# Eight products moved from the output stretch to the weights' stretch of a convolution and spectral-mix kernel

## The chip, the cores and the metric

One core of a Trainium2 chip. The metric is the device time of one execution in microseconds, as the median of several runs. A program on one core has no second die to compare with, so a run counts as slow only when it is over 1.5% above the fastest of its kernel. A ratio is the mean time of one kernel's fast runs over the mean time of the other's fast runs of the same rounds, so it is not quite the ratio of the medians beside it. Brackets hold its 95% interval.

## The reference

```python
# x: 8 x 3264 x 192.  u = causal convolution of x with 7 softmax-ed taps per head
X = np.fft.rfft(u, axis=1)                      # 64 modes are kept
Yr = einsum(Xr, w_r) - einsum(Xi, w_i)          # one 192 x 192 matrix per mode
Yi = einsum(Xr, w_i) + einsum(Xi, w_r)
y = np.fft.irfft(Y, n=S, axis=1)
v = u + y
out = v + np.maximum(v @ w_ch, 0.0)
```

## The kernel before

The kernel has three stretches. Input and convolution fill `xall` (u) and `cc` (u transposed, for the product with `w_ch`). Then 16 groups of weights are loaded, and each is multiplied as it lands. Then the output is made in double tiles, called items: 128 rows of positions by 2 x 2 x 192 values, in one of four PSUM buffers. Item n uses buffer n % 4. The parts that matter:

```python
    def c_part(n, ks=(0, 1)):            # twelve products: u @ w_ch of item n
        duo, zt = items[n]
        for k, (q, t) in enumerate(duo):
            for j in range(3) if k in ks else ():
                for i, r in enumerate(ROWS):
                    nc.tensor.matmul(zt[:, i, D * k:D * k + D], cc[r, q, 3 * t + j, :], wc[r, j, :],
                                     start=(k == 0 and j == 0), stop=False, skip_group_check=True)
    # m_part(n, 0): four products, adds y @ w_ch.   relu(n): ACT, in place in PSUM.
    # m_part(n, 1): four products, adds y.          finish(n): DVE adds u, POOL stores.
    ...
    for n in range(N + 1):
        if is_duo(n):
            m_part(n, 0)
            relu(n)
        if n + 2 < N and duos[n + 2] == ("h",):          # one tile of halves, made earlier
            nc.scalar.copy(out=items[n + 2][1]..., in_=halves...)
        if n + 1 < N and n > 0:
            if is_duo(n + 1):
                if duos[n + 1] != ("h",):
                    c_part(n + 1)
            else:
                ...                                      # a spectral item: y of the next quarter
        if is_duo(n - 1):
            m_part(n - 1, 1)
            finish(n - 1)
```

The names below follow this: c(n) is `c_part`, m(n,0) and m(n,1) are the first and second products of item n.

## Time and profile before

| | before |
|---|---|
| time, median of 3 runs | 179.58 us (179.52 to 180.19) |
| span of the profiled run, mean granted clock | 178.0 us, 0.984 |
| last group of weights used by PE | 106.93 us |
| first products of item 15 | 125.51 us |
| last store issued | 172.22 us |

Read it by stretches. Up to 107 us the weights set the pace, and PE has gaps. After it PE has none but the 0.25 us in front of the tile of halves, and everything else follows PE. The lines for both stand in the prediction. The rows of the last group of weights and of the last store cut the time into pieces that can be compared between kernels: what comes before the output, the output from the last group of weights to the last store issued (172.22 - 106.93 = 65.29 us), and what is left to land (178.0 - 172.22 = 5.8 us).

### The profile page before, as it was taken

To read this page: it belongs to the slowest core of one execution; us is meant where nothing else is said; L and a number is where in the kernel's file an instruction comes from. 1 tells how busy PE (TensorE), PEld (TensorE's weight loads), DVE (VectorE), ACT (ScalarE), POOL (GpSimd) and SP (SyncE) were. 2 spreads that over 40 slices of the span, in tenths; PEclk is the share of its full clock that TensorE was granted. 3 is DMA by queue.
4 is the path that set the end of the run, shared out by engine and by line. 5 is a ranking of instruction groups with operands and counts; after the bars stand their busy time and mean duration, and the time that the engine had idled before them with its cause. 6 is when DMAs were issued, how large, how long until landed. Compare 5 with 4: busy or idle time off the path is not lost.

```text
span 178.0 us, 6299 instructions
## 1 busy us (share of the span) xinstructions
PE 146.5 (82%) x2736; PEld 105.9 (59%) x2736; DVE 114.1 (64%) x163; ACT 99.5 (56%) x136; POOL 100.4 (56%) x155
## 2 busy tenths in 40 slices
PE   0047569999999999689967679999999999999930
PEld 0033346667666666467756556965777777777720
DVE  1878555675765576255454453796688888888870
ACT  8176653735553734365546355767766667766620
POOL 7999997867855624354226100035364766665760
PEclk9999987999999999999999999999999999999997
DMA  4999999999999999999999980296699899998894
GB/s 44 168 177 188 189 190 190 192 193 190 191 191 190 205 206 208 205 206 208 205 207 206 206 130 0 90 324 258 251 300 351 317 368 356 354 349 348 336 356 186
DMA packets 44331, 40.17 MB, mean 226 GB/s; under 512 B 28800, under 2 KB 40656, under 8 KB 44304
## 3 DMA queue, kind: packets, MB, share of 16 engines
q0 software_dynamic: 41136, 37.59, 106.0%
q1 hardware_dynamic: 3168, 2.19, 3.9%
q8 instruction: 21, 0.34, 0.7%
q14 instruction: 6, 0.05, 0.1%
HBM read 39.40 MB, written 20.05 MB: 334 GB/s over the span
## 4 chain that ended last, share of the span: by engine, by line
DMA 33%; POOL 32%; PE 16%; issue 13%; ACT 1%; POOLq 1%; DVE 1%; DVEq 0%
DMA arena<-in_moe_w_i_dram 19%; POOL out_dram L586 17%; POOL xall L151 10%; DMA xall<-in_x_dram 8%; DMA cc<-in_moe_w_i_dram 6%; PE z L307 4%; PE low L333 3%; PE za L522 2%; PE za L502 2%; POOL xall L221 1%; POOL arena L428 1%; PE zb L522 1%; PE zb L502 1%; ACT xall L325 1%; PE low L387 1%
## 5 line engine op out<-in xcount | busy, mean ns | idle before, releaser
L586 POOL DMA_DIRECT2D out_dram<-arena x45 | 33.9, 754 | 39.2 <-DVE arena L578 38.4
L151 POOL DMA_DIRECT2D xall<-in_x_dram x48 | 38.5, 813 | 6.7 <-DMA xall<-in_x_dram 4.6
L307 PE MATMUL z<-xall,band 64*64 64x192 bf16 (+3 forms) x816 | 27.8, 264 | 16.1 <-ACT band L195 10.5
L327 DVE CAST xall<-z 128x768 bf16<-128x768 f32 (+1 forms) x24 | 24.5, 1021 | 15.1 <-PE z L307 13.3
L307 PEld LDWEIGHTS <-band 64*64 64x64 bf16 x816 | 18.4, 111 | 24.8 <-ACT band L195 10.9
L325 ACT CAST xall<-z 128x768 bf16<-128x768 f32 (+1 forms) x24 | 20.4, 851 | 22.3 <-PE z L307 21.1
L502 PEld LDWEIGHTS <-cc 64*128 64x128 bf16 x600 | 26.2, 94 | 7.0 <-issue 1.2
L578 DVE TENSOR_TENSOR arena<-za,xall 128x768 f32<-128x768 f32 x26 | 24.8, 956 | 5.6 <-ACT zb L553 1.9
L553 ACT ACTIVATE za<-za 128x768 f32<-128x768 f32 (+1 forms) x27 | 21.0, 782 | 8.3 <-PE za L522 8.3
L578 DVE TENSOR_TENSOR arena<-zb,xall 128x768 f32<-128x768 f32 x23 | 21.9, 956 | 4.6 <-ACT za L553 1.8
L553 ACT ACTIVATE zb<-zb 128x768 f32<-128x768 f32 (+1 forms) x25 | 19.6, 782 | 8.4 <-PE zb L522 8.2
L333 PE MATMUL low<-xall,ftab 128*128 128x384 bf16 x100 | 21.7, 344 | 0.0
L387 PEld LDWEIGHTS <-xall 128*128 128x128 bf16 x300 | 18.7, 105 | 3.2 <-issue 0.3
L362 DVE COPY cc<-r 128x1024 bf16<-128x1024 bf16 (+2 forms) x18 | 11.2, 658 | 12.8 <-PE r L387 3.9
L502 PE MATMUL za<-wc,cc 64*128 64x192 bf16 x318 | 17.8, 243 | 0.0
L522 PE MATMUL za<-mixa,fsin 64*128 64x384 bf16 (+1 forms) x120 | 17.6, 304 | 0.0
L522 PE MATMUL za<-mixa,ftab 64*128 64x384 bf16 (+1 forms) x120 | 17.6, 304 | 0.0
L428 POOL DMA_DIRECT2D arena<-in_moe_w_r_dram x12 | 7.4, 615 | 15.4 <-PE low L439 10.3
L522 PE MATMUL zb<-mixa,ftab 64*128 64x384 bf16 (+1 forms) x100 | 15.6, 313 | 0.4 <-ACT zb L553 0.4
L502 PE MATMUL zb<-wc,cc 64*128 64x192 bf16 x282 | 15.6, 243 | 0.1
L522 PE MATMUL zb<-mixa,fsin 64*128 64x384 bf16 (+1 forms) x100 | 15.6, 313 | 0.0
L522 PEld LDWEIGHTS <-ftab 64*128 64x128 bf16 x220 | 11.0, 94 | 4.6 <-issue 1.7
(111 smaller groups left out, 184.2 us busy)
## 6 DMA issues: line engine op xcount, KB each, us to landing
out_dram<-arena POOLq DMA_DIRECT2D x45, 384.0 KB, 4.3
xall<-in_x_dram POOLq DMA_DIRECT2D x24, 192.0 KB, 7.4
xall<-in_x_dram POOLq DMA_DIRECT2D x16, 240.0 KB, 7.1
arena<-in_moe_w_r_dram POOLq DMA_DIRECT2D x12, 288.0 KB, 9.6
arena<-in_moe_w_i_dram POOLq DMA_DIRECT2D x12, 288.0 KB, 10.5
out_dram<-arena SPq DMA_DIRECT2D x9, 192.0 KB, 2.1
xall<-in_x_dram POOLq DMA_DIRECT2D x8, 144.0 KB, 7.1
cc<-in_moe_w_r_dram POOLq DMA_DIRECT2D x4, 288.0 KB, 11.5
```

What stands on the lines that cost most here:

```text
L151: nc.gpsimd.dma_start(out=xall[:, s0:s0 + nf, i, :], in_=src)
L307: mm = nc.tensor.matmul(ov[c], band[r, h, c.start + shift + 64 * (r is UP and c is LO): c.start + shift + 64 * (r is UP and c is LO) + 64] ...
L325: nc.scalar.copy(out=dst, in_=srcv)
L327: nc.vector.tensor_copy(out=dst, in_=srcv)
L333: nc.tensor.matmul(xp, ftab[:, t, :], xall[:, slot(q, t), :, :], start=(t == 0), stop=False, skip_group_check=True)
L362: nc.vector.tensor_copy(out=out, in_=in_)
L387: nc.tensor.transpose(tp[:, P * k:P * k + P], src, ident[:])
L502: nc.tensor.matmul(zt[:, i, D * k:D * k + D], cc[r, q, 3 * t + j, :], wc[r, j, :], start=(k == 0 and j == 0), stop=False, skip_group_check ...
L522: nc.tensor.matmul(zt[:, i, D * k:D * (k + w)], tabs[c][r, t, :], zw[r, q:q + w, c, QUARTERS[which], :], start=False, stop=end and k + w = ...
L553: nc.scalar.activation(out=zt[:, :, 0:w], in_=zt[:, :, 0:w], func=ACT.Relu)
L578: nc.vector.tensor_tensor(out=o[:, :, :].rearrange("p k (i d) -> p i k d", i=2), in0=zt[:, :, 0:2 * D].rearrange("p i (k d) -> p i k d", k=2),
L586: nc.gpsimd.dma_start(out=dst, in_=ov)
```

## The change

Intent: in the weights' stretch PE has time to spare, in the output it has none. So c of eight items is made in the first and used in the second. The results need room: each pair has one in `band` or a slice of the arena and one in the place of columns of `cc` that are used up. ACT brings each into PSUM two items ahead. The places for stores move to make room, and `cc` and `band`, which stores now leave from, are aligned to 256 B.

```diff
-    cc = sb("cc", [NQ, CB, P], BF16)
+    cc = sb("cc", [NQ, CB, P], BF16, align_bytes=256)
-    band = sb("band", [H, 2 * P], BF16)
+    band = sb("band", [H, 2 * P], BF16, align_bytes=256)
...
+    def c_ahead(n):
+        duo = duos[n]
+        zs = []
+        for i in range(2):
+            next_bank()
+            zs.append(ring[(tbank[0] - 1) % len(ring)])
+        ...                                    # the twelve products, into two banks of the ring
+        for i in range(2):
+            copy(AHEAD[n][:, i, :, :], zs[i][:, 0:2 * D].rearrange("p (k d) -> p k d", k=2))
...
+    FREED = {8: (16,), 9: (20,), 12: (24, 28), 13: (33, 41), 14: (37, 45)}
+    free = [in_cc[0], slices[4], slices[5], in_cc[1], slices[3]]
+    LATER = {11: (in_cc[2], in_cc[3]), 15: (in_band,), 23: (slices[0],), 32: (slices[1],), 40: (slices[2],)}
...
-    PLAN = (2, 2, 1, 2, 2, 2, 1, 2, 3, 3, 3, 3, 3, 3, 99)
+    PLAN = (2, 2, 3, 2, 3, 2, 2, 2, 3, 3, 3, 3, 99, 99, 99)
...
         some(PLAN[g], NT * (NQ - 1) if g < NW + NL - 1 else NT * NQ)
+        for n in FREED.get(g, ()):
+            c_ahead(n)
...
+        if n + 2 in AHEAD:
+            nc.scalar.copy(out=four(items[n + 2][1][:, :, 0:2 * D]), in_=AHEAD[n + 2])
...
-                if duos[n + 1] != ("h",):
+                if duos[n + 1] != ("h",) and n + 1 not in AHEAD:
                     c_part(n + 1)
```

More of the change, by code (lines that the diff above doesn't have):

```diff
@@ L95, in wbuf, with place, four @@
         return wts[g] if g < NW + NL else wts[(g - NW - NL) % NW]
-    NO = 6
     OB = 2 * 2 * 2 * D
-    outs = [arena[:, OB * i:OB * (i + 1)].bitcast(F32).rearrange("p (k d) -> p k d", k=2) for i in range(NO)]
-    assert NO * OB <= NW * WGB
-    outs.append(band[:, :, :].rearrange("p h c -> p (h c)")[:, 0:OB].bitcast(F32).rearrange("p (k d) -> p k d", k=2))
+    assert 6 * OB <= NW * WGB and OB == 12 * P
+    def place(a):
+        return a.bitcast(F32).rearrange("p (k d) -> p k d", k=2)
+    def four(a):
+        return a.rearrange("p k (i d) -> p k i d", i=2)
+    slices = [place(arena[:, OB * i:OB * (i + 1)]) for i in range(6)]
+    in_band = place(band[:, :, :].rearrange("p h c -> p (h c)")[:, 0:OB])
+    in_cc = [place(cc[:, q, t:t + 12, :].rearrange("p k s -> p (k s)")) for t in (0, 12) for q in range(2)]
+    ccf = cc[:, :, :, :].rearrange("p q (t j) s -> p q t (j s)", j=3).bitcast(F32)
     pos = [0]
@@ L495, in c_halves @@
             copy(halves[:, 2 * k:2 * k + 2, :], z[:, 0:2 * D].rearrange("p (a d) -> p a d", a=2))
+    def c_ahead(n):
[4 more added lines that the diff above has]
+            zs.append(ring[(tbank[0] - 1) % len(ring)])
+        for k, (q, t) in enumerate(duo):
+            for j in range(3):
+                for i, r in enumerate(ROWS):
+                    nc.tensor.matmul(zs[i][:, D * k:D * k + D], cc[r, q, 3 * t + j, :], wc[r, j, :],
+                                     start=(k == 0 and j == 0), stop=(k == 1 and j == 2), skip_group_check=True)
+        for i in range(2):
+            copy(AHEAD[n][:, i, :, :], zs[i][:, 0:2 * D].rearrange("p (k d) -> p k d", k=2))
     def c_part(n, ks=(0, 1)):
@@ L543 @@
         duos.insert(k, item)
-    buffers = []
-    for duo in duos:
-        buffers.append(NO if duo == ("h",) else sum(b < NO for b in buffers if b is not None) % NO
-                       if isinstance(duo, tuple) else None)
+    AHEAD = {}
+    for (n1, n2), p1 in zip(((16, 20), (24, 28), (33, 37), (41, 45)), [in_band] + slices):
+        (q, t1), (_, t2) = duos[n1][0], duos[n2][0]
+        AHEAD[n1], AHEAD[n2] = four(p1), ccf[:, q:q + 2, t1:t2 + 1:t2 - t1, :]
+        assert duos[n1] == ((q, t1), (q + 1, t1)) and duos[n2] == ((q, t2), (q + 1, t2)) and (q or t1 > 7)
+    FREED = {8: (16,), 9: (20,), 12: (24, 28), 13: (33, 41), 14: (37, 45)}
+    free = [in_cc[0], slices[4], slices[5], in_cc[1], slices[3]]
+    LATER = {11: (in_cc[2], in_cc[3]), 15: (in_band,), 23: (slices[0],), 32: (slices[1],), 40: (slices[2],)}
+    buffers = []
+    for n, duo in enumerate(duos):
+        for p in LATER.get(n, ()):
+            free.insert(0, p)
+        buffers.append(None)
+        if isinstance(duo, tuple):
+            buffers[n] = free.pop(0)
+            free.append(buffers[n])
     def relu(n):
@@ L556, in finish @@
         duo, zt = items[n]
-        o = outs[buffers[n]]
+        o = buffers[n]
         if duo[0] == "h":
```

## The prediction

> **What bounds the kernel now.** I read the mean clock first (0.984, nothing to correct), then the page's 40 slices and the chain that ended last. They show three stretches: input and convolution up to about 57 us, the weights up to 107 us, the output up to 176 us. I then asked for busy times by stretch, since the change takes work from the third and puts it in the second.
>
> ```profile
> core 0: us, PE busy (x) PEld busy (x) DVE busy (x) ACT busy (x) POOL busy (x), PEclk, DMA share, GB/s
> 80.00:90.00 10.00, 9.17 (x176) 7.13 (x176) 5.32 (x11) 5.07 (x10) 3.50 (x6) 1.00 1.21 206
> 90.00:100.00 10.00, 7.29 (x140) 6.33 (x138) 4.23 (x9) 5.09 (x8) 4.70 (x8) 1.00 1.21 207
> 100.00:107.00 7.00, 4.79 (x96) 3.51 (x97) 3.67 (x7) 3.48 (x7) 0.00 (x0) 1.00 0.92 151
> 141.00:146.00 5.00, 5.00 (x94) 3.95 (x92) 4.25 (x5) 3.44 (x5) 3.43 (x5) 1.00 0.98 374
> 156.00:161.00 5.00, 5.00 (x95) 3.95 (x92) 4.25 (x5) 3.56 (x5) 3.43 (x5) 1.00 0.89 342
> ```
>
> In the weights' stretch the DMA engines are full at 206 GB/s and PE has 0.83 + 2.71 + 2.21 = 5.75 us to spare. In the output PE never rests, while DVE is busy 4.25 of 5 us, ACT 3.5, and the DMA moves 342 to 374 GB/s at shares of 0.89 to 0.98. The chain that ended last names the stores on POOL there, but POOL waits 38.4 us for DVE, which waits for ACT, which waits for PE; the timeline of one tile shows the order.
>
> ```profile
> start us, us, engine line op out<-in xcount [idle before <-releaser]
> 149.79 0.33 PE L522 MATMUL za<-mixa,ftab 64*128 64x384 bf16 x2
> 149.95 0.33 PE L522 MATMUL za<-mixa,fsin 64*128 64x384 bf16 x2
> 150.05 0.96 DVE L578 TENSOR_TENSOR arena<-zb,xall 128x768 f32<-128x768 f32 x1 [0.19 <-ACT zb L553]
> 150.12 0.66 PE L502 MATMUL za<-wc,cc 64*128 64x192 bf16 x12
> 150.32 0.80 ACT L553 ACTIVATE za<-za 128x768 f32<-128x768 f32 x1 [0.35 <-PE za L522]
> ...
> 151.26 0.66 PE L502 MATMUL zb<-wc,cc 64*128 64x192 bf16 x12
> ```
>
> For double tile n, PE runs the four first-quarter products of n, the twelve products with c of n+1, and the four second-quarter products of n-1. From one twelve to the next is 151.26 - 150.12 = 1.14 us; start to start, the twelve take 150.61 - 150.12 = 0.49 us and each four 0.33 us, so 0.33 + 0.49 + 0.33 = 1.15 us. The stage goes at PE's pace.
>
> The kernel already has one tile whose product with c was made earlier, the tile of halves (item 14): ACT copies it into PSUM, and PE then adds to it. This is what the change makes of eight more.
>
> ```profile
> 122.05 0.33 PE L522 MATMUL za<-mixa,ftab 64*128 64x384 bf16 x2
> ...
> 122.64 0.80 ACT L553 ACTIVATE za<-za 128x768 f32<-128x768 f32 x1 [0.34 <-PE za L522]
> ...
> 123.38 0.80 ACT L643 COPY zb<-cc 128x768 f32<-128x768 f32 x1
> ...
> 124.23 0.36 PE L514 MATMUL zb<-mixa,ftab 64*64 64x384 bf16 x4 [0.25 <-ACT zb L643]
> ```
>
> PE stood 0.25 us waiting for that copy: the copy came after the ReLU of item 12 on ACT, and that ReLU waited for item 12's first products. So products, ReLU, copy, products is a chain of 124.23 - 122.05 = 2.18 us over two items, whatever PE has to do meanwhile.
>
> **What the Trainium skill says.** "Perfetto Trace Analysis", section Identifying the Most-Contended Engine, warns that a busy PE is not a PE at its roofline. Hence the starts above instead of the busy share. "ScalarE: Activation LUTs", section What ACT_TABLE_LOAD costs, gives an activation with immediates as 186 ns + 0.833 ns per element, with 93 ns of overlap back to back: 826 ns for 768 elements, 733 ns apart. The trace agrees: 0.78 to 0.80 us for one, 123.38 - 122.64 = 0.74 us apart. "DMA: Bandwidth & Descriptors", section How a descriptor splits into AXI transactions, says that a descriptor which doesn't start at a multiple of 256 B costs one more partial transaction. In the kernel before as built, the arena is aligned, and cc and band start 64 B past such a multiple. But of the stores only the halves come from there, and the weights' DMA time doesn't show it (below). The same page, section Where 436 GB/s comes from, puts the HBM limit of a core at about 358 GB/s; the trace shows 374 GB/s over 5 us at share 0.98, so I take 374 / 0.98 = 382 GB/s as the ceiling (an estimate from that row).
>
> **The change part by part.**
>
> Output stretch. Removed: twelve products with c for each of items 16, 20, 24, 28, 33, 37, 41, 45, so 8 x 0.49 = 3.9 us of PE. Added on ACT: eight copies of 128x768 from SBUF to PSUM at 0.74 to 0.80 us, 6.2 us. Built, the new order has each copy after the ReLU of the item two before, exactly as in the tile of halves. For a group of four items ACT then has 5 x 0.77 = 3.9 us and DVE 4 x 0.956 = 3.8 us, less than four tiles take, so neither is a bound by sum. The order is what matters. Let S be the start of item a-2's first products. Its ReLU starts at S + 0.53 (149.79 to 150.32), the copy 0.74 later, takes 0.80, and PE goes on 0.05 after it (124.18 to 124.23): item a starts at S + 2.12. The copy also needs the DVE addition of item a-4, which frees its PSUM buffer: it starts at S + 0.26 (150.05), ends at S + 1.22, and with the 0.09 us that ACT needed after DVE elsewhere (121.62 to 121.71) the copy starts at S + 1.31, making it S + 2.16. In the kernel before the two items take 2 x 1.145 = 2.29. PE's own work would allow 2.29 - 0.49 = 1.80. So each c made ahead saves about 0.15 us and not 0.49; the other 0.34 becomes a wait of PE for ACT. After the wait, ACT is one ReLU late, done at about S + 2.9, and the second products of that item come at S + 2.98: it just fits. Item 16 is better off, because its predecessors run at the slower pace around the halves: item 15's first products start at 125.51 and item 16's at 126.88 now; without the twelve PE would be there at 126.2 but the copy ends near 126.4, so about 0.43. Sum: 7 x 0.15 + 0.43 = 1.5 us.
>
> Weights' stretch. Added on PE: the same 3.9 us, in 5.75 us of idle time; it starts after group 8 of 16. Added copies of 128x384: ten on DVE at 0.63 us (the two copies of the halves took 1.26) and six on ACT at about 0.48. Both engines are idle half of this time. The transposes are only moved (three more before group 8, done sooner at the end). The weights' landing is set by the DMA. Loads are issued four groups ahead, 11.4 us, so a product with a group may run some 5 us late and starve nothing. What can hurt is the end:
>
> ```profile
> 104.08 0.46 PE L439 MATMUL low<-arena,mixa 128*16 128x192 bf16 x12 [0.72 <-DMA arena<-in_moe_w_i_dram]
> ...
> 105.85 1.26 DVE L362 COPY cc<-r 128x384 f32<-128x384 f32 x2 [1.59 <-PE r L492]
> ...
> 106.93 0.46 PE L439 MATMUL low<-arena,mixa 128*16 128x192 bf16 x12 [0.23 <-DMA arena<-in_moe_w_i_dram]
> ```
>
> Between the last two groups PE has 2.4 us. The new order puts 24 products (1.0 us) with four copies, then the halves' 24 (1.0 us) with two, into it; four of the six copies are DVE's, 4 x 0.63 = 2.5 us from about 105.1, to 107.6 instead of 107.1. I charge 0.2 us for the first output.
>
> Stores. The bytes are the same. Four tiles in 4 x 1.145 - 0.15 = 4.43 us are 1.573 MB at 355 GB/s, under 382. The kernel ends when the last store lands; with a fuller DMA I charge 0.2 us for a longer queue at the end. More places (five at first, up to eleven) remove no wait: none of DVE for a landed store is listed now. Alignment: I charge zero, since the weights' loads that go to unaligned cc took 11.45 us per four groups (72.17 to 83.62) and those to the aligned arena 11.4 to 11.9.
>
> Total: -1.5 + 0.2 + 0.2 = -1.1 us, so 179.6 becomes about 178.5.
>
> **Rivals.** First, the full gain: the copy lies wholly beside PE, 3.9 us come off, 175.7 us. For it: PE is the bound and ACT has the time by sum. Against it: the 0.25 us wait in front of the tile of halves, for the same order of instructions. Second, the DMA becomes the bound: then the saving ends at 1.573 MB / 382 GB/s = 4.12 us for four tiles, 0.46 per group, hardly another limit than the first rival's, and it binds only if that one is right; if the sustained ceiling is nearer the skill's 358, my 4.43 us per group is already all there is. Third, the weights' stretch overflows: PE runs late into the last group, 1 to 2 us are lost at once, and the sum is 179 to 180.5. Against it: 5.75 us idle for 3.9. Fourth, the wait cascades: the late ReLU also delays the second products of the item before, since I found only 0.1 us of slack; then each group loses 0.1 to 0.2 more and the time stays at 179.5.
>
> **Range and chances.** 178.5 with the first rival partly true gives 177.4 as the low end; the third or fourth gives 179.8 as the high end. Over 2% faster would be under 176.0, which needs the full gain and no loss at the end: 0.05. Over 2% slower, over 183.2, needs starved weights: 0.02.
>
> **What would show it.** A wait of PE for the ACT copy, eight times of about 0.3 us, 2.4 to 2.8 us in sum, and some 4.4 us for each four tiles, prove the chain; no such wait and 4.1 us prove the first rival. The last group of weights should still be used at 107 us, within 0.3; later proves the third. PE's second products waiting for a ReLU prove the fourth. I am wrong altogether if the copy from cc or band is much shorter than 0.80 us, or if the stores from cc and band move at another rate than those from the arena.

## The result, and the profile after

| | before | after |
|---|---|---|
| time, median of 6 runs | 179.78 us (179.52 to 180.19) | 178.88 us (178.60 to 179.41) |
| ratio | | 0.9954 [0.9933, 0.9975] |
| span of the profiled run, mean granted clock | 178.0 us, 0.984 | 177.1 us, 0.973 |
| last group of weights used | 106.93 us | 107.40 us |
| last store issued | 172.22 us | 171.19 us |
| from the one to the other | 65.29 us | 63.79 us |
| from the last store issued to the end | 5.8 us | 5.9 us |

The kernel is half a per cent faster, well within 2%. The result is correct. The two spans differ by 0.9 us, as the medians do, so the profiles are fit to explain it. The mean clocks differ by 0.011, but in every 5 us window of the output from 108 to 168 us the clock is 1.00 in both profiles.

First the busy times by stretch of the changed kernel, for the same windows as in the prediction (columns: window, length, busy time of PE, PEld, DVE, ACT, POOL with counts, clock, DMA share, GB/s):

```profile
80.00:90.00 10.00, 10.00 (x215) 8.26 (x210) 6.11 (x12) 6.46 (x10) 2.41 (x4) 1.00 1.21 206
90.00:100.00 10.00, 10.00 (x192) 8.46 (x189) 7.45 (x14) 6.08 (x11) 5.93 (x10) 1.00 1.21 206
100.00:107.00 7.00, 6.54 (x136) 5.11 (x133) 5.39 (x12) 3.89 (x8) 0.00 (x0) 1.00 1.01 167
141.00:146.00 5.00, 4.86 (x82) 3.77 (x78) 4.14 (x5) 4.01 (x6) 3.61 (x5) 1.00 0.98 373
```

PE's gaps in the weights' stretch are gone (9.17 + 7.29 + 4.79 = 21.25 us of 27 have become 26.54), and the DMA still moves its 206 GB/s: the products did go into idle time. In the output PE, which had no gap, now has one, 0.14 us in 5.

Where that gap comes from, the timeline of the changed kernel around item 20 shows. Item 18's first products start at 129.36; those of item 20, whose c was made ahead, at 131.47:

```profile
129.36 0.34 PE L546 MATMUL zb<-mixa,ftab 64*128 64x384 bf16 x2
...
129.90 0.80 ACT L593 ACTIVATE zb<-zb 128x768 f32<-128x768 f32 x1 [0.35 <-PE zb L546]
...
130.62 0.80 ACT L685 COPY za<-cc 128x768 f32<-128x768 f32 x1
...
130.99 0.34 PE L546 MATMUL zb<-mixa,fsin 64*128 64x384 bf16 x2
131.36 0.78 ACT L593 ACTIVATE zb<-zb 128x768 f32<-128x768 f32 x1
131.47 0.34 PE L546 MATMUL za<-mixa,ftab 64*128 64x384 bf16 x2
...
131.80 0.67 PE L526 MATMUL za<-wc,cc 64*128 64x192 bf16 x12
```

From 129.36 the ReLU comes 0.54 later, the copy 0.72 after that and ends at 131.42, and PE goes on at 131.47, 2.11 us after the start. The products before it end their starts at 130.99, one more step of 0.16 would be 131.15. So PE stands for 0.32 us. (The busy times count less, because the product that starts at 130.99 is given a modelled end of 131.33, which leaves 0.14 us.) Note that the list of waits does not name this: it has PE's matmul without a bracket, and the weight load of that line goes under "issue", 1.7 us before and 4.5 us after, which is the 2.8 us in sum that the prediction named as the mark of the chain. Here the end of the copy and the start of the products, 0.05 us apart, are the evidence, and the experiments have to say whether it is the cause.

Four items now take 4.41 us (items 20, 24 and 28 start at 131.47, 135.88 and 140.29) where they took 4 x 1.145 = 4.58.

The other end of the story is the last two groups of weights. The prediction shows that in the kernel before PE waited for both (104.08 and 106.93, 2.85 us apart). Now:

```profile
104.31 0.46 PE L448 MATMUL low<-arena,mixa 128*16 128x192 bf16 x12 [0.17 <-DMA arena<-in_moe_w_i_dram]
104.70 1.16 PE L516 MATMUL r<-wc,cc 64*128 64x192 bf16 x24
106.08 1.15 PE L501 MATMUL r<-wc,cc 64*64 64x192 bf16 x24 [0.22 <-DVE cc L371]
107.16 0.31 PE L468 MATMUL low<-ident,xs 128*96 128x128 bf16 x2
107.40 0.47 PE L448 MATMUL low<-arena,mixa 128*16 128x192 bf16 x12
```

The last group is no longer waited for. PE comes to it 3.09 us after the one before, because the 24 products with c (L516) and the 24 of the halves (L501) lie between, and the second set waits 0.22 us for a bank that DVE has to empty.

### The profile page after: what moved, and what is told of

The parts are those of the page before. It is cut to its first block, busy times and chain, and to the rows that moved or that the text cites.

```text
span 177.1 us, 6345 instructions
## 1 busy us (share of the span) xinstructions
PE 149.5 (84%) x2736; PEld 109.8 (62%) x2736; DVE 118.8 (67%) x173; ACT 106.5 (60%) x150; POOL 100.4 (57%) x155
## 4 chain that ended last, share of the span: by engine, by line
PE 36%; POOL 27%; DMA 17%; issue 13%; DVE 2%; ACT 2%; POOLq 1%; DVEq 0%; ACTq 0%
POOL out_dram L626 17%; DMA xall<-in_x_dram 12%; PE z L316 7%; POOL xall L160 7%; PE low L342 6%; DMA arena<-in_moe_w_i_dram 5%; PE r L396 4%; PE low L448 3%; PE r L385 3%; PE low L396 2%; PE za L546 2%; PE za L526 1%; PE low L468 1%; PE r L516 1%; DVE arena L618 1%
## 5 line engine op out<-in xcount | busy, mean ns | idle before, releaser
L626 POOL DMA_DIRECT2D out_dram<-arena x21 | 15.9, 757 | 25.9 <-DVE arena L618 25.1
L526 PEld LDWEIGHTS <-cc 64*128 64x128 bf16 x504 | 22.9, 94 | 5.3 <-issue 1.3
L626 POOL DMA_DIRECT2D out_dram<-cc x20 | 15.1, 755 | 8.9 <-DVE cc L618 6.9
L546 PE MATMUL za<-mixa,ftab 64*128 64x384 bf16 (+1 forms) x120 | 18.2, 305 | 1.0
L371 DVE COPY cc<-r 128x1024 bf16<-128x1024 bf16 (+2 forms) x23 | 13.9, 631 | 6.8 <-PE r L396 3.4
L546 PE MATMUL za<-mixa,fsin 64*128 64x384 bf16 (+1 forms) x120 | 18.2, 304 | 0.0
L546 PEld LDWEIGHTS <-ftab 64*128 64x128 bf16 x220 | 13.2, 94 | 7.1 <-issue 4.5
L546 PE MATMUL zb<-mixa,ftab 64*128 64x384 bf16 (+1 forms) x100 | 16.1, 313 | 0.4 <-ACT zb L593 0.4
L546 PE MATMUL zb<-mixa,fsin 64*128 64x384 bf16 (+1 forms) x100 | 16.1, 313 | 0.0
L526 PE MATMUL zb<-wc,cc 64*128 64x192 bf16 x282 | 15.9, 243 | 0.1
L369 ACT COPY cc<-r 128x1024 bf16<-128x1024 bf16 (+1 forms) x12 | 10.6, 881 | 8.0 <-PE r L396 4.6
L618 DVE TENSOR_TENSOR cc<-za,xall 128x768 f32<-128x768 f32 x13 | 12.4, 957 | 3.2 <-PE za L546 1.5
```

The source lines that it names most:

```text
L371: nc.vector.tensor_copy(out=out, in_=in_)
L546: nc.tensor.matmul(zt[:, i, D * k:D * (k + w)], tabs[c][r, t, :], zw[r, q:q + w, c, QUARTERS[which], :], start=False, stop=end and k + w = ...
L618: nc.vector.tensor_tensor(out=o[:, :, :].rearrange("p k (i d) -> p i k d", i=2), in0=zt[:, :, 0:2 * D].rearrange("p i (k d) -> p i k d", k=2),
L626: nc.gpsimd.dma_start(out=dst, in_=ov)
```

## The experiments

Twelve kernels ran, on three chips, four each, with 11 runs of the kernel before beside each four and six of each kernel. Edits are against the changed kernel unless said otherwise. "Wrong" means that the output is not the reference's.

| run | median, us | before beside it | ratio |
|---|---|---|---|
| e1, no ACT copies (wrong) | 179.04 | 179.89 | 0.9945 [0.9926, 0.9964] |
| e2, only the places and the alignment | 180.06 | 179.89 | 1.0013 [0.9995, 1.0030] |
| e3, no alignment | 184.08 | 179.89 | 1.0250 [1.0216, 1.0284] |
| e4, made ahead but not used | 181.59 | 179.89 | 1.0086 [1.0070, 1.0101] |
| e10, second products earlier | 181.04 | 179.93 | 1.0054 [1.0019, 1.0090] |
| e11, the same, no copies (wrong) | 178.71 | 179.93 | 0.9928 [0.9892, 0.9964] |
| e8, six items, earlier ones | 178.89 | 179.93 | 0.9939 [0.9901, 0.9978] |
| e9, six items | 179.02 | 179.93 | 0.9963 [0.9917, 1.0008] |
| e6, each copy twice | 185.06 | 180.14 | 1.0273 [1.0247, 1.0299] |
| e13, half additions (wrong) | 178.34 | 180.14 | 0.9910 [0.9879, 0.9942] |
| e12, half additions, no copies (wrong) | 177.92 | 180.14 | 0.9867 [0.9837, 0.9896] |
| e15, the changed kernel again | 179.18 | 180.14 | 0.9941 [0.9911, 0.9972] |

The theory: the ACT copy takes the place of c(a) on the path that sets the pace. The rivals: the wait is another one (a buffer that DVE gives back, a ReLU), or the DMA.

### e1: take the copies away

```diff
-        if n + 2 in AHEAD:
-            nc.scalar.copy(out=four(items[n + 2][1][:, :, 0:2 * D]), in_=AHEAD[n + 2])
```

> The changed kernel without the eight ACT copies of c into PSUM (the result is wrong on purpose). Chain theory (ReLU of item a-2, then the copy, then PE): PE no longer waits, item a starts 1.80 us after item a-2 instead of 2.11, eight times about 0.3 us come off, 2.4 us, so about 176.5 us; groups of four items take 4.1 us. Rival, DMA: if the stores already set the pace, at most 0.5 us comes off, 178.4 us. Rival, buffers: if PE waits for the DVE addition that frees the PSUM buffer rather than for the copy, nothing comes off, 178.9 us.

Measured: no gain, 0.9945 against 0.9954, as the third rival, the buffers, had it. My theory as I held it falls: with the copy gone, PE stands nearly as long. The timeline of e1 around item 20:

```profile
130.76 0.96 DVE L618 TENSOR_TENSOR arena<-za,xall 128x768 f32<-128x768 f32 x1 [0.19 <-ACT zb L593]
...
131.14 0.34 PE L546 MATMUL za<-mixa,ftab 64*128 64x384 bf16 x2
...
131.77 0.67 PE L526 MATMUL za<-wc,cc 64*128 64x192 bf16 x12
```

Item 20 does start 0.33 earlier, at 131.14, so the copy was what PE waited for there. But c(21), which should follow 0.33 later at 131.47, starts at 131.77. It goes into the buffer of item 17, and DVE is still adding from it until 130.76 + 0.96 = 131.72. Groups of four take 4.39 us. In the kernel before the twelve products of c(20) lay in between, and hid this. The list of waits moves in the same way: under "issue", the weight loads of L546, the products after the copy, are back from 4.5 to 1.7 us, and those of L526, the products c, go from 1.3 to 3.9.

### e2 and e3: the places and the alignment by themselves

e2 is the kernel before with the new places and the alignment, with no product made ahead and the old plan (the diff is against the changed kernel):

```diff
-    for (n1, n2), p1 in zip(((16, 20), (24, 28), (33, 37), (41, 45)), [in_band] + slices):
+    for (n1, n2), p1 in zip((), [in_band] + slices):
-    FREED = {8: (16,), 9: (20,), 12: (24, 28), 13: (33, 41), 14: (37, 45)}
+    FREED = {}
-    PLAN = (2, 2, 3, 2, 3, 2, 2, 2, 3, 3, 3, 3, 99, 99, 99)
+    PLAN = (2, 2, 1, 2, 2, 2, 1, 2, 3, 3, 3, 3, 3, 3, 99)
```

> The kernel before with only the new store places and the 256 B alignment: no product made ahead, old plan of the weights' stretch. My reading (no store place is waited for, alignment is worth nothing here): within 0.2 us of before, 179.6 to 180.0 us, landing of stores 4.3 us as before. Rival (aligned or more places speed the stores): 0.5 us or more faster, 179.2 us or less. Rival (stores from cc are slower): slower than 180.2.

Measured: 1.0013 [0.9995, 1.0030], nothing. Other places for stores gain nothing by themselves, as DVE waited for none.

e3 is the changed kernel without the alignment; as built, `cc` and `band` then start 64 B past a multiple of 256 B:

```diff
-    cc = sb("cc", [NQ, CB, P], BF16, align_bytes=256)
+    cc = sb("cc", [NQ, CB, P], BF16)
-    band = sb("band", [H, 2 * P], BF16, align_bytes=256)
+    band = sb("band", [H, 2 * P], BF16)
```

> The changed kernel with cc and band where the allocator put them before, 64 B past a multiple of 256 B, so that 24 of 45 stores leave from unaligned places. My reading: the DMA has room at 355 GB/s, so 178.8 to 179.2 us, within 0.3 us of the changed kernel. Rival (a partial transaction more per 768 B run costs DMA time): DMA share at the same GB/s up by 10 to 30 per cent for those stores, the DMA becomes the bound, 0.5 to 3 us slower, 179.5 to 182 us.

Measured: 184.08 us, 1.0250, so 5.2 us more than the changed kernel at 178.88. This is a miss: I had at most 0.3 us, and the rival, which was right in kind, at most 3. One window of the changed kernel, and the same of e3:

```profile
143.00:148.00 5.00, 4.86 (x86) 3.86 (x83) 4.32 (x5) 4.24 (x6) 3.72 (x5) 1.00 0.98 380
```

```profile
143.00:148.00 5.00, 4.86 (x84) 3.83 (x80) 4.17 (x5) 4.01 (x7) 3.46 (x5) 1.00 1.01 333
```

The page's lines of the stores, of the changed kernel and of e3 (last column: median time from issue to landing in us):

```profile
out_dram<-arena POOLq DMA_DIRECT2D x21, 384.0 KB, 4.6
out_dram<-cc POOLq DMA_DIRECT2D x20, 384.0 KB, 4.3
```

```profile
out_dram<-arena POOLq DMA_DIRECT2D x21, 384.0 KB, 7.1
out_dram<-cc POOLq DMA_DIRECT2D x20, 384.0 KB, 6.2
```

The DMA engines are as full, and move 333 GB/s in place of 380. The stores from the arena, which is aligned in both, land as late as the others, which fits their sharing the engines. PE is as busy in the one as in the other (4.86): the time is lost behind it, in the stores. Of the 5.3 us by which the span of e3 is longer, 3.85 come after the last store is issued (182.4 - 172.64 = 9.76 us in place of 5.91). So the alignment is needed because stores now leave from `cc` and `band`; in the kernel before only the tile of halves left from there. The loads of weights into unaligned `cc` had shown nothing, and I had argued from them.

### e4: pay for the products ahead, and don't use them

```diff
-        AHEAD[n1], AHEAD[n2] = four(p1), ccf[:, q:q + 2, t1:t2 + 1:t2 - t1, :]
+        AHEAD[n1], AHEAD[n2] = four(p1), four(p1)
...
-        if n + 2 in AHEAD:
-            nc.scalar.copy(out=four(items[n + 2][1][:, :, 0:2 * D]), in_=AHEAD[n + 2])
...
-                if duos[n + 1] != ("h",) and n + 1 not in AHEAD:
+                if duos[n + 1] != ("h",):
```

> The changed kernel that makes the eight products in the weights' stretch but does not use them: no ACT copies, and the output stretch makes all products as before (right result). It prices what the stretch pays. If filling the stretch delays the output's start, as the trace of the changed kernel suggests (last group used at 107.40 us instead of 106.93), 0.4 to 0.6 us slower than before: 180.2 to 180.4 us. Rival (the later start was only that profile's later DMA): within 0.2 us of before, 179.6 to 180.0 us.

Both results of a pair go to one place here, because the products c of the output still read the columns of `cc`.

Measured: 181.59 us, 1.7 us above the kernel before and more than expected. Its profiled run was the fastest, 1.2 us above in span. There the last group of weights was used at 107.44 us, 0.5 late, 3.10 us after the one before. Another 0.3 us comes from an addition that starts 0.31 us late (119.24 us, against 118.93 in the changed kernel), and 0.3 from a longer end (179.2 - 173.12 = 6.1 us). So e4 is not a clean measure of the cost in the weights' stretch; the 0.5 us that its slower runs have beyond this profile stay open.

### e10 and e11: the order of PE's work changed

If the wait is for a copy or a buffer, PE could do something else meanwhile. From item 15 on, the second products of the item before come ahead of c of the next:

```diff
+        if n >= 15 and is_duo(n - 1):
+            m_part(n - 1, 1)
+            finish(n - 1)
         if n + 1 < N and n > 0:
...
-        if is_duo(n - 1):
+        if n < 15 and is_duo(n - 1):
```

> The changed kernel with PE's order turned from item 15 on: the second products of item n-1 come before the product with c of item n+1, so a PSUM buffer is released 0.49 us earlier and needed 0.33 us later; copies as in the changed kernel (right result). Theory after the first four runs: two waits of nearly the same length stand one behind the other, the ACT copy (item a at S + 2.11) and the DVE addition that frees the buffer for the next c (shown by the run without copies). This run removes only the second, so the copy still holds PE: 178.7 to 179.1 us, like the changed kernel. Rival (the buffer alone holds PE): about 2 us faster, 177 us. Rival (the ReLU isn't ready in time for the earlier second products): over 1 us slower.

Measured: slower, 181.04 us, and the rival is right. In its timeline PE waits for ACT once more:

```profile
131.42 0.34 PE L546 MATMUL za<-mixa,ftab 64*128 64x384 bf16 x2
131.58 0.34 PE L546 MATMUL za<-mixa,fsin 64*128 64x384 bf16 x2
132.13 0.34 PE L546 MATMUL zb<-mixa,ftab 64*128 64x384 bf16 x2 [0.21 <-ACT zb L593]
```

The second products of item 19 need its ReLU, which ran after the copy (131.29 to 132.08). Groups of four take 4.77 us (131.42 to 136.19). e11 is the same without the copies:

> The same turned order without the eight copies (result wrong on purpose): both waits gone. Two-waits theory: groups of four items take 4.1 us, 8 x 0.3 = 2.4 us off, about 176.5 us; DMA share near 1. Rival (the DMA sets the pace at the present rate): 178.4 us or more, with groups of 4.1 us on PE but the last store landing no earlier. Rival (another wait): groups stay at 4.4 us.

Measured: 178.71 us, far from 176.5. With neither copy nor buffer in the way, the ReLU is the wait:

```profile
131.56 0.79 ACT L593 ACTIVATE za<-za 128x768 f32<-128x768 f32 x1
131.70 0.34 PE L546 MATMUL zb<-mixa,ftab 64*128 64x384 bf16 x2 [0.23 <-ACT zb L593]
```

Groups take 4.49 us (130.96 to 135.45). So in the turned order a third wait of nearly the same length comes up, the ReLU. It belongs to that order: in the kernel's own, c(a+1) comes before those second products, and e12 below shows no such wait. What stands behind one another in the changed kernel is two waits, the copy and the buffer that DVE gives back.

### e6: each copy twice

A dose of the suspected cost, with the right result:

```diff
-        if n + 2 in AHEAD:
+        for _ in range(2 if n + 2 in AHEAD else 0):
```

> The changed kernel with each of the eight copies issued twice (right result). If the copy is on the chain that sets the pace (first products, ReLU, copy, first products), each costs one more copy, 0.74 to 0.80 us, so 8 x 0.75 = 6 us more: about 184.9 us, groups of four at 5.15 to 5.2 us. If ACT had slack beside PE, much less: below 181 us.

Measured: 185.06 us against 179.18 for the changed kernel on the same chip (e15), 5.9 us more, as expected. In the timeline of e6 both copies lie in front of item 20:

```profile
131.21 1.64 ACT L685 COPY za<-cc 128x768 f32<-128x768 f32 x2
...
132.90 0.34 PE L546 MATMUL za<-mixa,ftab 64*128 64x384 bf16 x2 [0.98 <-ACT za L685]
```

PE starts 0.05 us after the second, and a group takes 5.24 us (132.90 to 138.14). The copy is on the path, with no slack. Together with e1 this says: the copy sets the pace, and the next limit is only 0.02 us per group below it.

### e12 and e13: take away the buffer's wait too

The addition of the item three before each of the eight is made over half of its width, so DVE gives the buffer of c(a+1) back 0.4 us sooner. The order of PE is the original one, in which c(a+1) still covers the ReLU.

```diff
+        hw = 1 if n + 3 in AHEAD else 2
-        nc.vector.tensor_tensor(out=o[...], in0=zt[...], in1=xall[...], op=ALU.add)
+        nc.vector.tensor_tensor(out=o[...][:, 0:hw], in0=zt[...][:, 0:hw], in1=xall[...][:, 0:hw], op=ALU.add)
```

e12 has no copies besides:

> The changed kernel without the eight ACT copies, and besides with the DVE addition of the item three before each of those items over half of its width only (wrong result on purpose: c is missing in eight tiles, half of eight others isn't written anew). Theory of three waits behind one another (copy on ACT, buffer given back by DVE, ReLU for the second products): this takes away the first two and leaves PE as long in front of the ReLU as before, so four items take PE's own 4 x 1.145 - 0.49 = 4.09 us in place of 4.41, and the kernel about 178.9 - 8 x 0.31 = 176.4 us. Rival, the DMA binds at about 380 GB/s or less: four items stay at 4.3 us or more, the DMA share is 0.98 to 1.00 in every window of the stage, and the time is 178 us or more. Rival, the ReLU binds all the same: 4.3 us or more with waits of PE for ACT in front of second products.

Measured: 177.92 us, 0.9867 [0.9837, 0.9896], the fastest of all, and 1.5 us above what I expected. The pace is as expected, 4.08 us per group. In the timeline of e12 around items 20 and 24 PE doesn't wait:

```profile
130.57 0.56 DVE L619 TENSOR_TENSOR arena<-za,xall 128x384 f32<-128x384 f32 x1 [0.18 <-ACT zb L593]
...
130.84 0.80 ACT L593 ACTIVATE zb<-zb 128x768 f32<-128x768 f32 x1 [0.35 <-PE zb L546]
130.96 0.33 PE L546 MATMUL za<-mixa,ftab 64*128 64x384 bf16 x2
...
131.28 0.66 PE L526 MATMUL za<-wc,cc 64*128 64x192 bf16 x12
...
131.78 0.33 PE L546 MATMUL zb<-mixa,ftab 64*128 64x384 bf16 x2
...
135.04 0.33 PE L546 MATMUL za<-mixa,ftab 64*128 64x384 bf16 x2
```

Item 20 starts at 130.96, item 24 at 135.04. The half addition ends at 131.13, before c(21) is due at 131.28, where the whole one of e1 ended after it. The ReLU of item 19 ends at 131.64, before that item's second products at 131.78.

The last store is issued at 168.74 us in place of 171.19. But the span ends at 176.0 in place of 177.1, because the end after it has grown from 5.9 to 7.3 us. The windows of e12 show why (last two columns):

```profile
153.00:158.00 5.00, 5.00 (x90) 3.89 (x86) 4.18 (x5) 4.00 (x6) 3.75 (x5) 1.00 1.01 373
158.00:163.00 5.00, 5.00 (x94) 3.90 (x92) 4.23 (x5) 3.31 (x5) 3.29 (x5) 1.00 1.02 381
```

The DMA is full from 143 us on, at 369 to 381 GB/s. Stores fall behind PE: the large ones from the arena land 5.5 us after their issue (median) in place of 4.6. Of the 2.45 us by which the last store is issued sooner, 1.35 are paid back at the end. This is read from the trace; no run takes load off the DMA to test it. This rival was right on the DMA and wrong on how it would show: I had it slow the groups down, but with up to eleven places for stores no group waits, and the queue takes it.

e13 has the half additions and keeps the copies:

> The changed kernel with its copies, and the half addition of the item three before each of the eight (wrong result on purpose). If the copy is the wait that ends last in the changed kernel, the earlier release of a buffer gives nothing: 178.7 to 179.0 us, groups of four still 4.4 us. If the release by DVE were what the copy waits for, 178 us or less.

Measured: 178.34 us, below what I expected by 0.4. Its profile has the pace of the changed kernel, 4.41 us per group (130.75 to 135.16), which is what the theory says. It is ahead by 0.67 us from the weights on: its last group but one was used at 103.65 us, that of e15 at 104.32. So the traces give no gain by the half additions, and a landing of the weights that differs from run to run. Why six runs should be 0.84 us below e15's is not settled; the intervals of their ratios overlap.

### e8 and e9: fewer items

Six items in place of eight, without those that were made in front of the last group. e9 leaves 41 and 45 out:

```diff
-    for (n1, n2), p1 in zip(((16, 20), (24, 28), (33, 37), (41, 45)), [in_band] + slices):
+    for (n1, n2), p1 in zip(((16, 20), (24, 28), (33, 37)), [in_band] + slices):
-    FREED = {8: (16,), 9: (20,), 12: (24, 28), 13: (33, 41), 14: (37, 45)}
+    FREED = {8: (16,), 9: (20,), 12: (24, 28), 13: (33, 37)}
```

> The changed kernel with six items made ahead (16, 20, 24, 28, 33, 37), two fewer. What 41 and 45 gain in the output (2 x 0.17 us) is lost, what they cost in the weights' stretch (some 0.45 us of late start in all) is mostly won back: 178.6 to 179.0 us, no difference. Rival (each made ahead is worth its whole 0.49 us of PE): 1 us slower, 179.9 us.

e8 takes items 6, 12, 16, 20, 24 and 28, the first two copied long before they are needed, into buffers that two spectral items have just left:

```diff
+    for (n1, n2), p1 in zip(((6, 12), (16, 20), (24, 28)), [in_band] + slices):
+    FREED = {8: (6,), 9: (12,), 12: (16, 20), 13: (24, 28)}
+    EARLY = {6: 2, 12: 8}
...
+        for a in AHEAD:
+            if EARLY.get(a, a - 2) == n:
+                nc.scalar.copy(out=four(items[a][1][:, :, 0:2 * D]), in_=AHEAD[a])
```

> Six items made ahead instead of eight: 6, 12, 16, 20, 24, 28. Items 6 and 12 sit in the PSUM buffers of the spectral items 2 and 8, which are free long before, so their copy is issued early and holds nothing (right result). Two-waits theory: 6 and 12 gain up to 0.49 us each (0.2 if the next item's buffer wait takes its place), 16 gains 0.47, the others 0.17 each, 1.4 to 2.0 us together, and two products fewer in the weights' stretch bring back most of the 0.45 us by which the output starts late: 177.9 to 178.5 us. Rival (only the number made ahead counts): slower than the changed kernel, 179.1 us or more.

Measured: 179.02 us for e9, at the upper end of what I expected, and 178.89 us for e8, above the expected 177.9 to 178.5: both the changed kernel's time. In both PE waits for the last group again, as in the first of these lines of e8's timeline:

```profile
106.69 0.46 PE L448 MATMUL low<-arena,mixa 128*16 128x192 bf16 x12 [1.39 <-DMA arena<-in_moe_w_i_dram]
...
122.12 0.67 PE L526 MATMUL za<-wc,cc 64*128 64x192 bf16 x12 [0.30 <-DVE cc L619]
```

That group is used 2.90 us after the one before in e8 and 2.88 in e9. That gives back 0.2 us, and the output stretch takes 64.0 us (e9) and 64.2 (e8) in place of 63.8, since fewer items save time in it. The two cancel. What e8 missed is the gain of 6 and 12: counted from the last group of weights, c(7) starts 0.18 us sooner than in e9 (8.74 against 8.92 us) and c(13) again only 0.18 (15.43 against 15.61), so 6 gained 0.18 us and 12 nothing. In front of c(7) and c(13), the second line, PE stands for the buffer that DVE gives back. No version is right and beats the changed kernel.

### e15: the changed kernel once more

> The changed kernel unaltered, once more beside the kernel before and the three others on the same chip, as the measure for them: 178.9 us, 0.9955 of the kernel before. Anything below 0.991 or above 0.999 would show that runs of different days of the chip can't be compared at half a per cent.

Measured: 0.9941 [0.9911, 0.9972], against 0.9954 the first time. Half a per cent came out again in rounds of their own.

## Why the prediction was right

The time was right to 0.4 us (178.5, measured 178.88). That alone says little, since the range of 177.4 to 179.8 takes in the kernel before (179.78) as well. What counts is the wait for the copy and its size, and they came as predicted. By its own terms:

| term | predicted, us | measured in the profiles, us |
|---|---|---|
| output, last group of weights to last store issued | -1.5 | 63.79 - 65.29 = -1.50 |
| late start | +0.2 | 107.40 - 106.93 = +0.47 |
| longer queue at the end | +0.2 | 5.91 - 5.78 = +0.13 |
| sum | -1.1 | -0.90 |

- **The saving per item.** I had the copy end at S + 2.12 to 2.16 and so 0.15 us saved in place of 0.49. Measured: S + 2.11, 4.41 us per group in place of 4.58, so 0.17. For item 16, 126.88 - 125.51 = 1.37 us after item 15 became 127.01 - 126.11 = 0.90, so 0.47 saved where I had 0.43. The chain was read from one 0.25 us wait in front of one tile of the kernel before; e6 shows that it is as tight as that, and e13 that the copy, not the buffer, ends last. That no other wait spoilt the number is luck: the next one, which I had not seen, lies 0.02 us per group below (e1).
- **The late start.** It was mis-sized in the trace, 0.47 for 0.2. But part of it is chance: the group before the last was itself used 0.23 us later (104.31 against 104.08). Over the ten profiles that have eight products ahead it is 103.65 to 104.61, mean 104.18. The part that PE's added work makes is 3.09 - 2.85 = 0.24 us, and it is steady: 3.09 to 3.17 us in those ten, 2.85 to 2.90 in the four that have fewer or none. With this part alone the sum would be -1.50 + 0.24 + 0.13 = -1.1. e4, which was to price this part by itself, came 1.7 us slower and leaves the rest of its cost open.
- **The first rival, the full gain.** It was refused with one argument, the wait for the copy. That is not enough, as e1 shows: without the copy there is no gain either. I had the numbers for the second wait, since I worked out when DVE frees a buffer, but only for the copy's own buffer, not for the one that c(a+1) needs. The twelve products of c(a) hid a buffer wait of 0.30 us (e1), and taking them away lays it open. A ReLU wait of 0.23 us (e11) comes up only when PE's order is turned as well.
- **The second rival, the DMA.** I wrote that it binds only if the first is right. e12 makes the first right, and by its trace the DMA binds: the last store is issued 2.5 us sooner, and the span is 1.1 us shorter. The estimate of 382 GB/s as the ceiling held over 25 us (369 to 381). The Trainium skill's 358 in "DMA: Bandwidth & Descriptors", section Where 436 GB/s comes from, is 716 GB/s divided by two cores; for this program, which runs on one core, it was no limit.
- **The third and fourth rivals.** The third, an overflow of 1 to 2 us, came as 0.24. The fourth, a cascade, did not come: item 19's second products started at 132.29, 2.93 us after S, where I had 2.98. e10 shows how near it was, since a swap that gives 0.49 us of cover away makes it real at once.
- **The alignment.** I charged zero, and e2 measures zero. The reason I gave was wrong. I concluded from loads that alignment does not count here. But a load writes to `cc`, and a store reads from it. For stores it counts 5.2 us (e3), and the charge was zero only because the change had put it right. I had named it as what would make me wrong altogether, if stores from `cc` moved at another rate, and left it at that; the changed kernel's own new places were the reason for the added `align_bytes`, and that should have been asked.

## What to carry to other kernels

When work is taken out of an engine that never rests, ask which waits that work was hiding, all of them and not only the first: list, for each instruction after the hole, when its other inputs will be there. Here two waits cost the same to within 0.02 us per four items (4.41 and 4.39), a third (4.49) came up when PE's order was turned to get round the second, and behind them stood the DMA at a share of up to 0.98, so that even with both out of the way 3.9 us less work of PE were worth 2.2 us (180.14 to 177.92). And when a buffer gets a new use as the source of stores, look at its start address before looking at anything else.

## What the Trainium skill lacked or had wrong

- "DMA: Bandwidth & Descriptors", section Where 436 GB/s comes from: it says of HBM to SBUF transfers that "the HBM side (~358) binds", and gives the figure as the share of one of two cores. That both must be streaming stands in another section of the page, Measured. Here, with a program on one core, it doesn't bind: stores of 768-byte rows ran at 380 GB/s over 5 us in the changed kernel, and at 369 to 381 over 25 us in e12, at a DMA share of 0.99 to 1.02.
- The same page, section How a descriptor splits into AXI transactions: confirmed in direction for stores, but it counts transactions and beats and gives no time for them. By its rule a row of 768 B, if it is one descriptor, is three transactions aligned and four when it starts 64 B late, 24 beats and 26. (The prediction's "one more" holds for such rows and not for all: the 96 B example there stays at one.) With 24 of the 45 large stores unaligned the full DMA moved 333, 305 and 347 GB/s in three windows of e3, and 370, 377 and 373 in the same windows of e12: 14% more time per byte, so by my estimate 0.137 x 45 / 24 = 26% per unaligned store, if the windows hold the two kinds in that mix. That is nearer to the ratio of transactions (33%) than to that of beats (8%).
- The same section speaks of reading only (the bytes before the start "are fetched but unused") and does not say what an unaligned destination costs. The loads of weights into an unaligned place took 11.45 us for four groups, those into an aligned one 11.4 to 11.9, so nothing was seen there. Their rows have another size too (1152 B in SBUF), and no run separates size from direction.
- "ScalarE: Activation LUTs", section What ACT_TABLE_LOAD costs: its figures, 826 ns for 768 elements alone and 733 apart, are for an ACTIVATE; it gives none for a plain copy. The copies from SBUF to PSUM took 797 to 804 ns each, about 3% less, with the next ReLU 0.74 us after the copy's start (130.62 to 131.36).
